# Attention in one tiling of four 64x64 tiles, with the softmax division inside the transposes

## The chip, the cores and the metric

One core of a Trainium2 chip runs the whole program. The metric is the device time of one execution in microseconds: median 962.74 us before the change, three runs between 958.96 and 964.65.

## The reference

The program is one attention layer and two mixture-of-experts layers. The change lies in the attention; q, k and v have 4 batches x 8 heads, 576 positions and 64 elements per head.

```python
scores = scale * np.matmul(q, k.transpose(0, 1, 3, 2))
log_f = np.log(np.clip(f, 0.0001, 1.0))
cum = np.cumsum(log_f, axis=-1)
decay = cum[:, :, :, None] - cum[:, :, None, :]
scores = np.where(causal, -1000000000.0, scores + decay)
scores = scores - np.max(scores, axis=-1, keepdims=True)
attn = np.exp(scores)
attn = attn / (np.sum(attn, axis=-1, keepdims=True) + 1e-09)
return np.matmul(attn, v).astype(np.float32)
```

## The kernel before, in words

The 32 heads are taken in 16 pairs p; the two heads of a pair lie in the two halves of the 128 partitions. The queries of a head are five tiles (QT, L29): tile 0 has 64 rows, tiles 1 to 4 have 128, and tile i needs only the first 64, 192, 320, 448 or 576 keys. 1600 key columns a head in all.

**Scores, qk (L119).** Per tile and head, an f32 product of 64 contraction rows fills 64x128 of TensorE's array, and a bf16 product (f32 for pair 0) adds the decay of the keys. An f32 product appears in the profile as two records, a bf16 product and an f32 transpose as one. VectorE takes the scores out of PSUM, adds the causal mask and finds the row's extreme (L151; tile 4 in two halves of 288 columns), ScalarE makes the exponential in place and the row sum (L159).

**Transposes, tr (L166).** The attention weights are transposed in blocks of 128x128 by TensorE's transpose (L175, L185, L190, L192), in four groups g, and copied out by ScalarE and VectorE (L177, L196, L198). **Products with v, av (L201)** use 128x64 or 64x64 of the array and gather in two PSUM tiles.

**Division.** rb (L209) inverts the row sums on VectorE, rt (L215) transposes them, writes them to DRAM (rd, L224) and reads them back as a broadcast over the partitions (rb, L226). xout (L228) copies the result out of PSUM on ScalarE and VectorE, multiplies it by that broadcast on GpSimd (L235) and splits it into two parts for the next layer (L237, L238).

**Order.** run (L240) writes TensorE's order out by hand: within iteration p, the transposes and products with v of pair p stand between the scores of pair p+1. The orders of the other engines and of the DMA queue on SyncE are a planner's. The load of q and k for pair p+2 and the weight fetches of the next layer are issued only after the broadcast of pair p (issue_after, L255). Every second iteration from p=3 to p=13, a block of the next layer's weights is decoded (L319) on ScalarE, VectorE and GpSimd; two small router weights (gw, L443) are loaded by code that stands behind the attention.

PSUM holds four score tiles, two transpose tiles and two result tiles, of one bank each.

Of the kernel before, what the change touches and what calls it, by code (L numbers as in the profile page):

```python
# [29 lines left out]
EO = {1: 0, 3: 192, 2: 640, 4: 960}  # L30
TQ = [None, (1, 2, 3, 4), (2, 3, 4), (3, 4)]
AV = [[(0, 0, 64, 0, 256, 0, 64), (0, 64, 64, 0, 256, 1, 0)],
# [3 lines left out]
NP = B * H // 2  # L36
PE = mybir.EngineType.PE


class Attention:  # L40
    def __init__(self, tc, ctx, cst, io, xth, xtl):
        self.tc, self.nc, self.cst, self.io = tc, tc.nc, cst, io
        self.xth, self.xtl = xth, xtl
        nc = self.nc
        dr = ctx.enter_context(tc.tile_pool(name="at_dr", bufs=1, space=DRAM))
        self.cd = dr.tile([B * H, 3, S], BF16, name="cd")
        self.rd = [dr.tile([10, 128], F32, name=f"rd{p}") for p in range(NP)]
        self.raw = ctx.enter_context(tc.tile_pool(name="at_raw", bufs=3))
        self.vp = ctx.enter_context(tc.tile_pool(name="at_v", bufs=2))
        self.ep = ctx.enter_context(tc.tile_pool(name="at_e", bufs=4))  # L50
        self.ap = ctx.enter_context(tc.tile_pool(name="at_a", bufs=2))
        self.xp = ctx.enter_context(tc.tile_pool(name="at_x", bufs=3))
        self.sm = ctx.enter_context(tc.tile_pool(name="at_sm", bufs=6))
        fix = ctx.enter_context(tc.tile_pool(name="at_fix", bufs=1))
        self.ps_s = ctx.enter_context(tc.tile_pool(name="ps_s", bufs=4, space=PSUM))
        self.ps_t = ctx.enter_context(tc.tile_pool(name="ps_t", bufs=2, space=PSUM))
        self.ps_x = ctx.enter_context(tc.tile_pool(name="ps_x", bufs=1, space=PSUM))
        self.e0 = [fix.tile([128, 128], F32, name=f"e0_{i}") for i in range(4)]
        self.dk = [fix.tile([128, S], BF16, name=f"dk{i}") for i in range(2)]
        self.neg = fix.tile([128, 128], BF16, name="neg")  # L60
        self.rs = [fix.tile([128, 10], F32, name=f"rs{i}") for i in range(2)]
        self.rr = [fix.tile([128, 32], F32, name=f"rr{i}") for i in range(2)]
        for t in self.e0 + self.dk[::-1]:
# [4 lines left out]
        for t in self.rr:  # L68
            nc.gpsimd.memset(t, 0.0)
        self.mark = [None, None, None]  # L70
        self.R, self.V, self.E, self.T = {}, {}, {}, {}
# [11 lines left out]
    def decay(self, ft, cum, c8, pc):  # L83
# [12 lines left out]
        nc.vector.tensor_sub(pc[:, 2], cum, pc[:, 1])  # L96
        nc.sync.dma_start(out=self.cd, in_=pc)

    def warm(self, n):
        z = self.e0[0]  # L100
        tp = self.ps_t.tile([128, 512], F32, name="ps_t")
        for i in range(n):
            self.nc.tensor.matmul(tp[:, :128], z, z, start=True, stop=True)
# [6 lines left out]
    def vload(self, p):  # L110
        nc = self.nc
        v = self.V[p] = self.vp.tile([128, 2, 7, D], F32, name="v")
        nc.sync.dma_start(out=v, in_=self.io["vL"][2 * p:2 * p + 2].rearrange("a p j d -> p a j d"))

    def rows(self, p):
        ins = self.nc.sync.dma_start(out=self.dk[p % 2][61:67], in_=self.cd[2 * p:2 * p + 2].rearrange("a r s -> (a r) s"))
        self.mark[2] = self.mark[2] or ins

    def qk(self, p, i, later=False):  # L119
# [4 lines left out]
        rs = self.rs[p % 2]  # L124
        if p not in self.E:
            self.E[p] = [self.ep.tile([128, 1536], F32, name="e") for _ in range(2)]
        es = ([self.e0[2 * (p % 2) + a] for a in range(2)] if i == 0 else
              [e[:, EO[i]:EO[i] + w] for e in self.E[p]])
        mask = self.cst["mask"]
        off = 448 + m - w if m == 128 else 512  # L130
        b = 128 - m
        prev = [None, None]
        for lo, hi in [(0, w)] if w <= 512 else [(0, w // 2), (w // 2, w)]:
            n = hi - lo
            ps = [self.ps_s.tile([128, 512], F32, name="ps_s") for _ in range(2)]
            for c in range(2):
                for a in range(2):
                    h = 64 * a
                    x, y = r[h:h + 64, 0, q0:w], r[h:h + 64, 1, lo:hi]
                    if c and p:  # L140
                        x, y = self.neg[h:h + 64, :m], d[h:h + 64, lo:hi]
                    elif c:
                        x, y = self.cst["sel"][h:h + 64, :m], self.c8[h:h + 64, lo:hi]
                    nc.tensor.matmul(ps[a][b:, :n], x, y, start=c == 0, stop=c == 1, tile_position=(h, b))  # L144
            for a in range(2):
                mx = self.sm.tile([128, 1], F32, name="mx")
                o, x, y = es[a][b:, lo:hi], ps[a][b:, :n], mask[b:, off + lo:off + hi]
                if i in (1, 2):
                    o, x, y = (t.rearrange("p (b k) -> p b k", k=64) for t in (o, x, y))
                    o = o[:, ::-1]  # L150
                nc.vector.tensor_tensor_reduce(  # L151
                    out=o, in0=x, in1=y, scale=-0.125,
                    scalar=BIGF if prev[a] is None else prev[a][b:], op0=ALU.add, op1=ALU.min, accum_out=mx[b:],
                )
                prev[a] = mx
        def exps():
            for a in range(2):
                c = a * 5 + i
                nc.scalar.activation(es[a][b:, :w], es[a][b:, :w], ACTF.Exp, bias=prev[a][b:], scale=-1.0,  # L159
                                     accum_out=rs[b:, c:c + 1])  # L160

        if later:
            return exps
        exps()

    def tr(self, p, g):  # L166
        nc = self.nc
        ident = self.cst["ident"]
        es = self.E[p]
        if g == 0:  # L170
            tp = self.ps_t.tile([128, 512], F32, name="ps_t")
            for a, e in enumerate(es):
                for c, o in enumerate((EO[3] - 64, EO[4] - 64)):
                    c += 2 * a
                    nc.tensor.transpose(tp[:, 128 * c:128 * (c + 1)], e[:, o:o + 128], ident)  # L175
            th = self.ap.tile([128, 512], F32, name="ath0")
            self.mark[0] = nc.scalar.activation(th, tp, ACTF.Copy)  # L177
            self.T[g, 0], self.T[g, 1] = th[:, :256], th[:, 256:]
            return
        tps = [self.ps_t.tile([128, 512], F32, name="ps_t") for _ in range(2)]  # L180
        n = 320 if g == 3 else 512
        k0 = 128 * g - 64
        if g == 3:
            for a, tp in enumerate(tps):
                nc.tensor.transpose(tp[:, 256:320], self.e0[2 * (p % 2) + a][64:, :], ident[64:, 64:],  # L185
                                    tile_position=(64, 0))
        for tp, e in zip(tps, es):
            for c, i in enumerate(TQ[g]):
                o = EO[i] + (QT[i][0] - k0 if i < 3 else k0)
                nc.tensor.transpose(tp[:, 128 * c:128 * (c + 1)], e[:, o:o + 128], ident)  # L190
            if g == 2:
                nc.tensor.transpose(tp[:, 384:512], e[:, EO[4] + 448:EO[4] + 576], ident)  # L192
        for a, tp in enumerate(tps):
            th = self.ap.tile([128, n], F32, name=f"ath{g}")
            if g == 3 or a:
                self.mark[1] = nc.vector.tensor_copy(th, tp[:, :n])  # L196
            else:
                self.mark[0] = nc.scalar.activation(th, tp[:, :n], ACTF.Copy)  # L198
            self.T[g, a] = th

    def av(self, p, g):  # L201
        nc = self.nc
        v = self.V[p]
        for j, k0, k, o, n, x, d0 in AV[g]:
            for a in range(2):
                nc.tensor.matmul(self.X[x][64 * a:64 * a + 64, d0:d0 + n], v[k0:k0 + k, a, j],  # L206
                                 self.T[g, a][k0:k0 + k, o:o + n], start=g == 0, stop=g == 3, tile_position=(k0, 64 * a))

    def rb(self, p):  # L209
# [868 lines left out]
```

## Time and profile before

| what | value |
|---|---|
| profiled execution, device time | 968.61 us |
| its span, first to last instruction | 966.8 us |
| median of three runs | 962.74 us |
| TensorE busy | 935.5 us, 97% of the span |
| VectorE, ScalarE, GpSimd busy | 61%, 43%, 24% |
| mean granted TensorE clock | 0.986 of 2.4 GHz |
| attention, until the next layer's matmuls follow each other | 207 us |

A row with a start and a length is one or several instructions of one form in order of time; in brackets stands how long the engine was idle before it and what it waited for. A group is all instructions of a line and shape, with their busy time and mean length. Matmuls overlap: the next one starts before the record of the last one ends, so that the distance between starts tells more than the length.

### The profile page before, as it was taken

What the parts mean: (1) busy time and instruction counts of PE and PEld (TensorE: products, weight loads), DVE (VectorE), ACT (ScalarE), POOL (GpSimd) and SP (SyncE); (2) the same over time, 40 slices, a digit from 0 to 9 for tenths busy, and PEclk for the clock granted to TensorE, in tenths of its full rate; (3) what the DMA queues carried; (4) which work ended last, traced back from release to release, by engine and by line L of the source; (5) the groups of instructions that cost most, each with busy time, mean ns of one, the idle gap of its engine ahead of it and who ended that gap; (6) DMA issues with size and microseconds to landing.
All of it is one profiled execution on the core that took longest, in us unless ns stands there. A gap on an engine that the chain in (4) does not pass through costs nothing.

```text
span 966.8 us, 16505 instructions
## 1 busy us (share of the span) xinstructions
PE 935.5 (97%) x6288; PEld 843.8 (87%) x6288; DVE 593.3 (61%) x1420; ACT 411.9 (43%) x903; POOL 232.9 (24%) x205
## 2 busy tenths in 40 slices
PE   7999999899999999999999999999899999999995
PEld 5655665489999999999999999899799999999995
DVE  6677777546586469459458445677785566465421
ACT  5676767534442132123123122333364465465431
POOL 1244444433121011012012000000112654345122
PEclk9999999999999999999999999999799999999998
DMA  5444444312132012013002000011485666566300
GB/s 161 117 136 136 132 131 139 105 56 66 44 110 65 1 47 85 1 29 104 1 22 87 1 1 1 33 67 55 157 263 171 202 236 202 169 197 218 112 35 30
DMA packets 53088, 94.83 MB, mean 98 GB/s; under 512 B 5954, under 2 KB 27086, under 8 KB 53007
## 3 DMA queue, kind: packets, MB, share of 16 engines
q1 hardware_dynamic: 47503, 79.58, 27.1%
q0 software_dynamic: 5504, 14.17, 4.3%
q8 instruction: 50, 0.82, 0.4%
q14 instruction: 31, 0.25, 0.1%
HBM read 84.10 MB, written 10.16 MB: 97 GB/s over the span
## 4 chain that ended last, share of the span: by engine, by line
PE 73%; DVE 9%; issue 7%; DMA 5%; POOL 2%; ACT 2%; SPq 0%; POOLq 0%; DVEq 0%; ACTq 0%
PE ps_g L377 26%; PE ps_y L395 13%; PE m_psy L698 8%; PE m_psg L683 7%; PE ps_s L144 5%; PE ps_t L190 3%; DVE dt L327 2%; PE avx L206 2%; PE avy L206 2%; DMA raw<-w 1%; DMA rd<-rt 1%; DMA qk<-qk 1%; ACT e L159 1%; PE m_pst L648 1%; PE rt_ps L534 1%
## 5 line engine op out<-in xcount | busy, mean ns | idle before, releaser
L377 PE MATMUL ps_g<-xth,w 128*128 128x384 f32 (+1 forms) x1184 | 309.0, 331 | 0.0
L377 PEld LDWEIGHTS ps_g<-xth,w 128*128 128x128 f32 x1184 | 213.2, 188 | 0.6
L377 PE MATMUL ps_g<-xtl,w 128*128 128x384 f32 (+1 forms) x592 | 196.4, 332 | 0.0
L395 PE MATMUL ps_y<-hh,w 128*128 128x384 f32 (+1 forms) x592 | 160.9, 333 | 2.2 <-DVE y L401 2.2
L698 PE MATMUL m_psy<-h2h,w 128*128 128x304 f32 x512 | 115.9, 309 | 0.0
L683 PE MATMUL m_psg<-ygh,w 128*128 128x304 f32 x512 | 115.1, 307 | 0.4 <-ACT ygh L650 0.4
L340 POOL TENSOR_TENSOR w<-ds,w 128x512 fp32r<-128x512 f32 x36 | 49.2, 1368 | 262.9 <-ACT w L339 262.4
L377 PEld LDWEIGHTS ps_g<-xtl,w 128*128 128x128 f32 x592 | 111.3, 188 | 0.1
L395 PEld LDWEIGHTS ps_y<-hh,w 128*128 128x128 f32 x592 | 107.1, 188 | 4.3 <-DVE y L401 4.0
L610 DVE TENSOR_TENSOR w<-raw,w 128x1024 fp32r<-128x1024 f32 x64 | 76.6, 1222 | 42.2 <-ACT w L609 21.8
L159 ACT ACTIVATE e<-e,mx 128x320 f32<-128x320 f32 (+4 forms) x160 | 88.0, 552 | 33.0 <-DVE mx L151 32.5
L395 PE MATMUL ps_y<-hl,w 128*128 128x384 f32 (+1 forms) x296 | 97.9, 331 | 0.0
L384 ACT ACTIVATE hh<-hs 128x384 fp32r<-128x384 f32 (+1 forms) x74 | 38.2, 516 | 134.6 <-DVE hs L383 134.6
L382 DVE SCALAR_TENSOR_TENSOR hs<-hs,ps_g 128x384 f32<-128x384 f32 (+1 forms) x74 | 40.0, 540 | 83.5 <-ACT hs L381 83.5
L151 DVE CUSTOM_DVE_ANT_0 e<-ps_s,mask 128x320 f32<-128x320 f32 (+4 forms) x160 | 62.7, 429 | 43.6 <-PE ps_s L144 33.6
L698 PEld LDWEIGHTS m_psy<-h2h,w 128*128 128x128 f32 x512 | 86.8, 191 | 0.4
L683 PEld LDWEIGHTS m_psg<-ygh,w 128*128 128x128 f32 x512 | 85.6, 189 | 0.6 <-ACT ygh L650 0.5
L609 ACT ACTIVATE w<-raw 128x1024 fp32r<-128x1024 f32 x64 | 67.5, 1058 | 40.7 <-PE m_psg L683 17.6
L381 ACT ACTIVATE hs<-ps_g 128x384 f32<-128x384 f32 (+1 forms) x74 | 35.3, 478 | 102.2 <-PE ps_g L377 102.1
L401 DVE TENSOR_TENSOR y<-ps_y,y 128x384 f32<-128x384 f32 (+1 forms) x124 | 67.0, 541 | 19.1 <-PE ps_y L395 18.2
L698 PE MATMUL m_psy<-h2l,w 128*128 128x304 f32 x256 | 78.2, 306 | 0.0
L683 PE MATMUL m_psg<-ygl,w 128*128 128x304 f32 x256 | 77.3, 302 | 0.0
(308 smaller groups left out, 1514.1 us busy)
## 6 DMA issues: line engine op xcount, KB each, us to landing
raw<-w SPq DMA_DIRECT2D x64, 512.0 KB
qk<-qk SPq DMA_DIRECT2D x16, 576.0 KB
v<-vL SPq DMA_DIRECT2D x16, 448.0 KB
raw<-mg SPq DMA_DIRECT2D x12, 512.0 KB
raw<-mv SPq DMA_DIRECT2D x12, 512.0 KB
raw<-mo SPq DMA_DIRECT2D x12, 512.0 KB
rb<-rd SPq DMA_DIRECT2D x16, 288.0 KB
yd<-yr SPq DMA_DIRECT2D x18, 256.0 KB
```

Of the source, the lines that this page charges most:

```text
L144: nc.tensor.matmul(ps[a][b:, :n], x, y, start=c == 0, stop=c == 1, tile_position=(h, b))
L151: nc.vector.tensor_tensor_reduce(out=o, in0=x, in1=y, scale=-0.125, scalar=BIGF if prev[a] is None else prev[a][b:], op0=ALU.add, op1=ALU. ...
L159: nc.scalar.activation(es[a][b:, :w], es[a][b:, :w], ACTF.Exp, bias=prev[a][b:], scale=-1.0, accum_out=rs[b:, c:c + 1])
L340: nc.gpsimd.tensor_sub(lo, s3, hi.bitcast(F32))
L377: nc.tensor.matmul(ps[:, :n], w[:, k, fs], x[:, k], start=(k == 0 and c == 0), stop=(k == 3 and c == 2))
L382: nc.vector.scalar_tensor_tensor(s[:, :n], s[:, :n], 1.0, pss[0][:, :n], op0=ALU.add, op1=ALU.mult)
L395: nc.tensor.matmul(ps[:, :n], w[:, f, ds], h[:, f, :n], start=(f == 0 and c == 0), stop=(f == 1 and c == 2))
L401: nc.vector.tensor_add(y, ps[:, :n], y)
L609: nc.scalar.activation(hi, r, ACTF.Copy)
L610: nc.vector.tensor_sub(lo, r, hi.bitcast(F32))
L683: nc.tensor.matmul(ps[:, :C], w[:, k, fs], x[:, k], start=(k == 0 and c == 0), stop=(k == 3 and c == 2))
L698: nc.tensor.matmul(self.P[e][d][:, :C], w[:, f, ds], h[:, f], start=(u == 0 and f == 0 and c == 0), stop=(u == 3 and f == 1 and c == 2))
```

## The change

All matmuls of the attention now use a quarter of the array, 64x64, at one of four places (row half, column half). A score product of 128 queries becomes two of 64. A transposition becomes an ordinary f32 product of a 64x64 block of weights with a 64x64 diagonal that holds the reciprocal row sums (inv), so that it divides as well; blocks that the mask empties are left out: 45 blocks a head, in three groups (KB), where the row halves have 6 and 8, 7 and 8, 8 and 8 blocks, times two heads on the two column halves. Products with v alternate heads between row halves: av runs twice per group, with swap 0 in iteration p and with swap 1 in iteration p+1.

Score PSUM is two tiles of two banks (one for each of tiles 0 to 3, both for tile 4), transposes and results have one tile of two banks each. Tile 4 of the scores is one VectorE instruction of 576 columns. The DRAM round trip (rd, rb), rt and the GpSimd multiply are gone; GpSimd makes the diagonals in two steps (columns 0 to 5 for tiles 4, 3, 2; columns 6 to 9 for tiles 1 and 0). v is loaded as 288 KB a pair and not 448. The order of all five engines is now written out by hand, and the scores of tile 4 for pair p+2 close iteration p. The decode steps are spread over two iterations, ScalarE's logarithm table is asked for at the start, and the router weights are loaded within the next layer.

```diff
--- before.py
+++ after.py
...
+EO = [1536, 0, 192, 512, 960]
+COL = [8, 6, 4, 2, 0]
+KB = [(3, 4, 7, 8), (1, 2), (0, 5, 6)]
 NP = B * H // 2
-PE = mybir.EngineType.PE
+ENG = mybir.EngineType
+def rows_of(kb):
+
+    return [list(range((kb + 2) // 2, 5)) + [0] * (kb == 0), list(range(max((kb + 1) // 2, 1), 5))]
...
+        self.ps_s = pool("ps_s", 2, space=PSUM)
+        self.ps_t = pool("ps_t", 1, space=PSUM)
+        self.ps_x = pool("ps_x", 1, space=PSUM)
...
+        one = self.sm.tile([128, 1], F32, name="one")
+        nc.vector.memset(one, 1.0)
+        nc.scalar.activation(one, one, ACTF.Ln)
...
-        nc.vector.tensor_sub(pc[:, 2], cum, pc[:, 1])
+        nc.gpsimd.tensor_sub(pc[:, 2], cum, pc[:, 1])
+        self.load(1)
+        self.vload(0)
         nc.sync.dma_start(out=self.cd, in_=pc)
...
+        v = self.V[p] = self.vp.tile([128, 9, D], F32, name="v")
+        self.nc.sync.dma_start(out=v, in_=self.io["vL"][p])
...
+        wide = w > 512
+        n = w // 2 if wide else w
+        ps = [self.ps_s.tile([128, 2, 512], F32, name="ps_s") for _ in range(1 + wide)]
+        for j in range(1 + wide):
+            ks = slice(j * n, j * n + n)
...
+                    h = slice(64 * a, 64 * a + 64)
+                    o = ps[a][:, j] if wide else ps[0][:, a]
+                    for b in range(0, m, 64):
+                        x, y = r[h, 0, q0 + b:q0 + b + 64], r[h, 1, ks]
+                        if c and p:
+                            x, y = self.neg[h], d[h, ks]
+                        elif c:
+                            x, y = self.cst["sel"][h], self.c8[h, ks]
+                        nc.tensor.matmul(o[b:b + 64, :n], x, y, start=c == 0, stop=c == 1, tile_position=(64 * a, b))
+        mask = self.cst["mask"][:m, 448:512] if i == 0 else self.cst["mask"][:, 576 - w:576]
+        for a in range(2):
+            mx = self.M[p, i, a] = self.sm.tile([128, 1], F32, name="mx", bufs=10)
+            o = self.E[p][a][:m, EO[i]:EO[i] + w]
+            x, y = (ps[a][:, :, :n] if wide else ps[0][:m, a, :n]), mask
+            if wide:
+                o, y = (t.rearrange("p (j n) -> p j n", j=2) for t in (o, y))
+            nc.vector.tensor_tensor_reduce(out=o, in0=x, in1=y, scale=-0.125, scalar=BIGF, op0=ALU.add, op1=ALU.min,
+                                           accum_out=mx[:m])
+
+    def exp(self, p, i):
+        m = QT[i][1]
+        w = QT[i][0] + m
+        for a in range(2):
+            c = COL[i] + a
+            e = self.E[p][a][:m, EO[i]:EO[i] + w]
+            self.nc.scalar.activation(e, e, ACTF.Exp, bias=self.M.pop((p, i, a))[:m], scale=-1.0,
+                                      accum_out=self.rs[p % 2][:m, c:c + 1])
+
+    def inv(self, p, c0, c1):
+        nc = self.nc
+        if p not in self.D:
+            self.D[p] = (self.dp.tile([128, 10, 64], F32, name="d"), self.sm.tile([128, 10], F32, name="r"),
+                         self.sm.tile([128, 10], F32, name="rr"))
+        d, r, rr = self.D[p]
+        nc.gpsimd.tensor_scalar_add(r[:, c0:c1], self.rs[p % 2][:, c0:c1], 1e-9)
+        nc.vector.reciprocal(rr[:, c0:c1], r[:, c0:c1])
+        sh = [128, c1 - c0, 64]
+        nc.gpsimd.tensor_tensor(d[:, c0:c1], self.cst["id2"].unsqueeze(1).to_broadcast(sh),
+                                rr[:, c0:c1].unsqueeze(2).to_broadcast(sh), op=ALU.mult)
+
+    def tr(self, p, g, ps=None):
+        nc = self.nc
+        tp = (ps or self.ps_t).tile([128, 2, 512], F32, name="ps_s" if ps else "ps_t")
+        es, d = self.E[p], self.D[p][0]
+        jobs, self.at = [[], []], {}
+        for kb in KB[g]:
+            for r, tiles in enumerate(rows_of(kb)):
+                self.at[kb, r] = len(jobs[r]), tiles
+                jobs[r] += [(kb, i) for i in tiles]
+        for n in range(8):
+            for r in range(2):
+                if n >= len(jobs[r]):
+                    continue
+                kb, i = jobs[r][n]
+                h = slice(64 * r, 64 * r + 64)
+                for c in range(2):
+                    a = (c + kb) % 2
+                    o = EO[i] + 64 * kb
+                    nc.tensor.matmul(tp[64 * c:64 * c + 64, r, 64 * n:64 * n + 64], es[a][h, o:o + 64],
+                                     d[h, COL[i] + a], start=True, stop=True, tile_position=(64 * r, 64 * c))
...
+        ns = [64 * len(j) for j in jobs]
+        for r in range(2):
+            o, x = th[:, r, :ns[r]], tp[:, r, :ns[r]]
+            if r == (g != 2):
+                nc.scalar.activation(o, x, ACTF.Copy)
             else:
+                nc.vector.tensor_copy(o, x)
+
+    def av(self, p, g, swap):
...
+        for kb in sorted(KB[g], key=lambda kb: (kb // 2 if g else (kb - 1) // 2, kb)):
+            for r in range(2):
+                t = r ^ swap
+                n0, tiles = at[kb, t]
+                if not tiles:
+                    continue
+                a = (r + kb) % 2
+                h, lo = slice(64 * r, 64 * r + 64), tiles[0] - 1
+                hi, w = lo + len(tiles), self.W[t, a]
+                for u0, u1 in list(self.parts(lo, hi, w)):
+                    m0 = 64 * (n0 + u0 - lo)
+                    nc.tensor.matmul(x[64 * a:64 * a + 64, t, 64 * u0:64 * u1], v[h, kb],
+                                     th[h, t, m0:m0 + 64 * (u1 - u0)], start=not w, stop=swap == 1 and kb in (5, 6),
+                                     tile_position=(64 * r, 64 * a))
+                    w.update(range(u0, u1))
...
-        nc.scalar.activation(xt[:, :320], ax, ACTF.Copy)
-        nc.vector.tensor_copy(xt[:, 320:], ay[:, :256])
-        nc.gpsimd.tensor_mul(xt, xt, self.rbt)
+        nc.vector.tensor_copy(xt[:, 64:].rearrange("p (s t q) -> p t s q", s=4, t=2),
+                              x[:, :, :256].rearrange("p t (s q) -> p t s q", s=4))
+        nc.vector.tensor_copy(xt[:, :64], x[:, 0, 256:320])
...
+        with self.tc.manual_schedule(engines={ENG.PE, ENG.Activation, ENG.DVE, ENG.Pool, ENG.SP}):
+            self.decay(*dec)
+            self.rows(1)
             self.warm(WARM0)
+            for i in (4, 3, 2, 1, 0):
                 self.qk(0, i)
+                self.exp(0, i)
+            self.warm(WARM1)
+            self.inv(0, 0, 6)
+            self.qk(1, 4)
             for p in range(NP):
                 nx = p + 1 < NP
+                if p + 2 < NP:
+                    self.load(p + 2)
+                hook("load", p)
+                self.inv(p, 6, 10)
+                self.tr(p, 0)
+                if nx:
+                    self.exp(p + 1, 4)
+                    self.qk(p + 1, 3)
+                self.tr(p, 1)
+                if nx:
+                    self.exp(p + 1, 3)
+                hook("a", p)
+                if p:
+                    for g in range(3):
+                        self.av(p - 1, g, 1)
+                    self.xout(p - 1)
+                if nx:
+                    self.vload(p + 1)
+                    self.qk(p + 1, 2)
+                    self.exp(p + 1, 2)
+                hook("b", p)
+                self.tr(p, 2)
+                self.av(p, 0, 0)
+                self.av(p, 1, 0)
+                if nx:
+                    self.qk(p + 1, 1)
+                    self.inv(p + 1, 0, 6)
+                    self.exp(p + 1, 1)
+                self.av(p, 2, 0)
+                if nx:
+                    self.qk(p + 1, 0)
+                    self.exp(p + 1, 0)
                 if p + 2 < NP:
                     self.rows(p + 2)
+                    self.qk(p + 2, 4)
+            for i in range(2):
+                tp = self.warm(2)
+                if i == 0:
+                    nc.vector.tensor_copy(self.sm.tile([128, 10], F32, name="r")[:, :1], tp[:, 0, :1])
+            for g in range(3):
+                self.av(NP - 1, g, 1)
+            self.xout(NP - 1)
...
+        if eng:
+            eng.tensor_scalar(s, s, 2.0 ** -30, None, op0=ALU.is_ge)
         nc.vector.scalar_tensor_tensor(t, hv, -0x40000000, t, op0=ALU.bitwise_and, op1=ALU.bitwise_or)
+        yield
         nc.vector.scalar_tensor_tensor(t, lv, 29, t, op0=ALU.logical_shift_right, op1=ALU.bitwise_or)
+        yield
         tf = t.bitcast(F32)
         if eng:
-            eng.tensor_scalar(s, s, 2.0 ** -30, None, op0=ALU.is_ge)
             eng.tensor_mul(s, s, tf)
...
+                def hook(at, p):
+                    if at == "load":
+                        if p == 1:
+                            cst.rest()
+                        if p == H0:
+                            todo.extend(m1.parts(0))
+                        if p >= H0 and (p - H0) % 2 == 0 and todo:
+                            todo[0] = m1.fetch(todo[0][0]), *todo[0][1:]
+                    if at == "b" and p == H0:
+                        cst.split()
+                    if at == "a" and p > H0 and (p - H0) % 2 and todo:
                         dec.append(m1.decode(*todo.pop(0), eng=nc.gpsimd))
+                        next(dec[0])
+                    elif dec:
+                        for _ in zip(range(1), dec[0]):
+                            pass
+                        if at == "b" and (p - H0) % 2 == 0:
                             for _ in dec.pop():
                                 pass
 
...
+                        if (i, f) in ((3, 0), (8, 0)):
+                            with tc.issue_after(m1.mark[0].ins), tc.issue_after(m1.mark[1].ins):
+                                next(gates, None)
```

## Rows read from the trace of the kernel before

**Rows 1.** Busy time and granted clock in three stretches of time.
```profile
core 0: us, PE busy (x) PEld busy (x) DVE busy (x) ACT busy (x) POOL busy (x), PEclk, DMA share, GB/s
16.00:22.00 6.00, 5.08 (x22) 2.61 (x23) 2.14 (x9) 3.23 (x12) 0.00 (x0) 0.72 0.29 70
92.71:104.10 11.39, 11.39 (x100) 7.08 (x99) 7.66 (x32) 8.03 (x26) 3.49 (x3) 1.00 0.43 119
182.00:188.00 6.00, 3.10 (x27) 1.88 (x29) 1.88 (x9) 2.47 (x10) 1.45 (x2) 1.00 0.18 58
```

**Rows 2.** TensorE in order of time: start us, length us.
```profile
16.02 0.77 PE L175 MATMUL ps_t<-cst,e 128*128 128x128 f32 x3 [1.19 <-ACT e L159]
...
30.21 0.66 PE L175 MATMUL ps_t<-cst,e 128*128 128x128 f32 x4
...
52.86 0.55 PE L175 MATMUL ps_t<-cst,e 128*128 128x128 f32 x3
...
184.09 0.66 PE L175 MATMUL ps_t<-cst,e 128*128 128x128 f32 x4
...
187.79 0.81 PE L144 MATMUL ps_s<-qk 64*128 64x320 f32 x4 [2.90 <-DMA qk<-qk]
...
199.94 0.66 PE L175 MATMUL ps_t<-cst,e 128*128 128x128 f32 x4
...
207.06 0.44 PE L377 MATMUL ps_g<-xtl,w 128*128 128x384 f32 x1
```

**Rows 3.** TensorE in order of time, inside one iteration.
```profile
92.71 0.43 PE L206 MATMUL avx<-ath,v 64*64 64x256 f32 x2
92.73 0.43 PE L206 MATMUL avy<-ath,v 64*64 64x256 f32 x2
92.98 0.38 PE L206 MATMUL avx<-ath,v 64*64 64x256 f32 x2
...
103.08 1.09 PE L190 MATMUL ps_t<-cst,e 128*128 128x128 f32 x8
104.10 0.43 PE L206 MATMUL avx<-ath,v 64*64 64x256 f32 x2
```

**Rows 4.** Groups by form, 0 to 210 us: xcount | busy, mean.
```profile
L206 PE MATMUL avy<-ath,v 128*64 128x256 f32 x192 | 33.6, 385 | 1.6 <-DVE ath L196 1.6
...
L235 POOL TENSOR_TENSOR xt<-xt,rb 128x576 f32<-128x576 f32 x15 | 21.2, 1410 | 123.6 <-DMA rb<-rd 52.3 <-ACT xt L233 27.7 <-ACT e L159 22.3
...
L159 ACT ACTIVATE e<-e,mx 128x320 f32<-128x320 f32 x32 | 17.8, 556 | 21.1 <-DVE mx L151 20.9
...
L151 DVE CUSTOM_DVE_ANT_0 e<-ps_s,mask 128x320 f32<-128x320 f32 x32 | 14.5, 487 | 24.4 <-PE ps_s L144 24.4
...
L331 POOL TENSOR_SCALAR ds<-ds 128x512 f32<-128x512 f32 x6 | 9.3, 1548 | 0.5
...
L332 POOL TENSOR_TENSOR ds<-ds,dt 128x512 f32<-128x512 f32 x6 | 7.6, 1274 | 1.0 <-DVE dt L328 0.5
...
L206 PE MATMUL avy<-ath,v 128*64 128x128 f32 x64 | 6.2, 273 | 0.0
...
L328 DVE SCALAR_TENSOR_TENSOR dt<-raw,dt 128x512 int32<-128x512 int32 x6 | 4.8, 796 | 0.2
```

**Rows 5.** VectorE in order of time, in the same iteration.
```profile
103.18 0.63 DVE L151 CUSTOM_DVE_ANT_0 e<-ps_s,mask 128x448 f32<-128x448 f32 x1
...
103.73 0.62 DVE L151 CUSTOM_DVE_ANT_0 e<-ps_s,mask 128x448 f32<-128x448 f32 x1
...
104.28 0.69 DVE L196 COPY ath<-ps_t 128x512 f32<-128x512 f32 x1
```

**Rows 6.** SyncE's DMA issues in order of time, last iterations of the attention.
```profile
163.98 0.63 SPq L224 DMA_DIRECT2D rd<-rt  x1
176.26 0.51 SPq L226 DMA_DIRECT2D rb<-rd  x1
176.83 0.46 SPq L108 DMA_DIRECT2D qk<-qk  x1
177.38 0.28 SPq L116 DMA_DIRECT2D dk<-cd  x1
```

**Rows 7.** VectorE in order of time, at the start.
```profile
10.85 0.19 DVE L445 CAST gw<-gw 128x64 fp32r<-128x64 f32 x1 [0.56 <-DMA gw<-wo]
```

More of the change, by code (lines that the diff above doesn't have):

```diff
@@ L67, in __init__ @@
             nc.gpsimd.memset(t, 1.0)
[L68 to L71, printed above, removed]
+        self.R, self.V, self.E, self.M, self.D, self.T, self.X = {}, {}, {}, {}, {}, {}, {}
     def decay_load(self, pool):
@@ L123, in qk @@
         w = q0 + m
-        rs = self.rs[p % 2]
         if p not in self.E:
[L126 to L135, printed above, removed]
+            self.E[p] = [self.ep.tile([128, 1600], F32, name="e") for _ in range(2)]
@@ L144, in qk @@
[L144 to L166, printed above, removed]
-        nc = self.nc
[L168 to L196, printed above, removed]
-            else:
-                self.mark[0] = nc.scalar.activation(th, tp[:, :n], ACTF.Copy)
-            self.T[g, a] = th
@@ L202, in av @@
+    def av(self, p, g, swap):
         nc = self.nc
         v = self.V[p]
[L204 to L209, printed above, removed]
-        nc = self.nc
-        r = self.sm.tile([128, 10], F32, name="r")
-        nc.vector.tensor_scalar_add(r, self.rs[p % 2], 1e-9)
-        nc.vector.reciprocal(self.rr[p % 2][:, :10], r)
@@ L215, in rt @@
-    def rt(self, p):
-        nc = self.nc
-        self.X = self.ps_x.tile([128, 320], F32, name="avx"), self.ps_x.tile([128, 384], F32, name="avy")
-        tp = self.X[1][:32, 256:]
-        nc.tensor.transpose(tp, self.rr[p % 2], self.cst["ident"])
-        rt = self.sm.tile([32, 128], F32, name="rt")
-        nc.scalar.activation(rt, tp, ACTF.Copy)
-        rb = self.rbt = self.xp.tile([128, S], F32, name="rb")
-        d = self.rd[p]
-        nc.sync.dma_start(out=d, in_=rt[:10])
-        d = d.rearrange("(a i) q -> a (i q)", a=2)[:, 64:]
-        self.mark[2] = nc.sync.dma_start(out=rb, in_=d.unsqueeze(1).to_broadcast([2, 64, S]))
+        if p not in self.X:
+            self.X[p] = self.ps_x.tile([128, 2, 512], F32, name="avx")
+            self.W = {(t, a): set() for t in range(2) for a in range(2)}
@@ L238, in xout, with run @@
         nc.gpsimd.tensor_sub(self.xtl[:, f, sl], xt, self.xth[:, f, sl].bitcast(F32))
-    def run(self, extra, pool):
+    def run(self, hook, pool):
+        nc = self.nc
         dec = self.decay_load(pool)
@@ L243, in run @@
         self.cst.load()
-        self.decay(*dec)
-        self.vload(0)
-        self.load(1)
-        self.rows(1)
-        with self.tc.issue_after(self.mark[2].ins):
-            self.vload(1)
-        with self.tc.manual_schedule(engines={PE}):
+        with self.tc.manual_schedule(engines={ENG.PE, ENG.Activation, ENG.DVE, ENG.Pool, ENG.SP}):
+            self.decay(*dec)
+            self.rows(1)
             self.warm(WARM0)
-            for i in (2, 3, 4, 1, 0):
+            for i in (4, 3, 2, 1, 0):
@@ L277, in run @@
-                for g in range(2, 4):
-                    self.av(p, g)
+                if p + 2 < NP:
[14 more added lines that the diff above has]
+                    self.xout(p - 1)
@@ L414 @@
 P0, P1 = 1, 1
[L415 removed]
+H0, WARM0, WARM1 = 2, 10, 3
 BLK0 = [4, 5, 6, 7, 8, 10, 12, 14, 16, 20, 22]
```

125 lines of the change are left out of this document (39 added, 86 removed), and 3 rows, old and new, of the table AV.

## Prediction

> **What bounds the kernel now.** I read busy time by stretch first. In an iteration in mid attention TensorE is busy without a gap for all of 11.39 us, while VectorE, ScalarE and GpSimd are busy 7.66, 8.03 and 3.49 us [rows 1]. Iterations are told apart by their first transposes: the first takes 14.2 us (16.02 to 30.21), the two after it 11.3 each, the eleven from 52.86 to 184.09 take 131.2 us or 11.93 each, since every second one also decodes weights, the fifteenth takes 15.85, and 7.1 us go from the last one's start to the next layer's steady stream [rows 2]. Then I read why the late ones are longer. SyncE holds its queue 12.3 us between writing the reciprocals (163.98) and reading them back (176.26), and the loads of q and k stand behind that [rows 6]; TensorE then waits 2.90 us for them [rows 2] and is busy 3.10 of 6 us [rows 1].
>
> Inside an iteration I read distances between starts. Two av records of one tile, 256 columns, stand 0.27 us apart: 0.21 of streaming and 0.055 of weights that nothing hides [rows 3]. From 128 to 256 columns a record grows by 112 ns [rows 4], close to two cycles a column at 2.4 GHz, the level that a granted clock of 1.00 means; so an f32 product of two records streams 1.67 ns a column. Eight transposes and a change of tile shape take 1.02 us (103.08 to 104.10), 0.15 more than eight steps of the 109 ns that I read as one of them [rows 3]. By these the streams of an iteration are: scores 3.33 us (1600 columns, f32 plus a bf16 record that I take as one cycle a column), transposes 2.83 (26), products with v 2.67. That is 8.8; the other 2.6 are some thirteen changes of shape and exposed weight loads.
>
> **The change, TensorE's own work.** Four 64x64 products start within 20 ns of one another today (92.71 to 92.73) and their second records together [rows 3], so I take four at once. Scores keep 3.33. The new transposes are 8 deep in each group: 8 products x 2 records x 56 ns (53 of stream) = 0.9 us, 2.7 for three. Products with v: the fullest tile has 14 blocks of 64 columns with swap 1 (1.5 us) and 8, then 6, with swap 0 (0.85 and 0.64). With small rests the iteration is 0.9 tr0, 0.93 scores 3, 0.9 tr1, 1.5 av, 0.67 scores 2, 0.9 tr2, 0.85 av, 0.4 scores 1, 0.64 av, 0.17 scores 0, 1.2 scores 4: 9.06 us, 2.3 under today's. No shape changes.
>
> **What the hand order makes late.** With TensorE this short, chains through the other engines end later. Prices: a 448-column extreme on VectorE every 0.55 us (103.18, 103.73), a 512-column copy 0.69 long [rows 5]; about 1.05 ns a column between the 320-column form's 487 ns [rows 4] and 448, so 0.68 for 576, 0.28 for 192, 0.15 for 64. A hand-over costs 0.1, from TensorE 0.2, an estimate.
> - Before tr1: after scores 4, VectorE does two extremes (0.2+1.36), then the reciprocal that stands behind them (0.25); GpSimd's multiply of 256 columns follows. The trace has no such small one. Bounds: nothing, and the 1.27 of 512 columns; at the 2.1 ns a column between 512 and 576 [rows 4] I take 0.7. With hand-over 2.57, against 1.95 of tr0 and scores 3: a stall of 0.6.
> - Before the last av: from the end of the swap-1 av, xout's two copies (0.2, then 0.6 and 0.14: the 0.69 copy of [rows 5] less its overlap with the next; both are on VectorE now), an extreme (0.42), two exponentials of tile 2 (0.18+1.12 [rows 4]), ScalarE's copy (0.6, a little under VectorE's 0.69): 3.3, against 2.82 on TensorE. A stall of 0.5.
> - Scores 4 need both score tiles, so the extremes of tile 0 first: 0.65.
>
> With 0.1 before scores 3 the iteration is 10.9 us, 0.4 under today's 11.3. GpSimd loses the 1.41 multiply and gains 0.7 and 1.0; it has room, except in decode iterations. In the odd ones the 1.55 comparison [rows 4] stands on GpSimd ahead of the reciprocals, which hold VectorE's queue and so the extremes of tile 0 and scores 4; what scores 4 wait for anyway covers half of it: 0.8. In the even ones a VectorE step of 0.8 [rows 4] stands before the reciprocal: 0.75. So 11.7 there, against 11.93.
>
> SyncE: the two round-trip issues and their wait go. The load of v now waits for av of the pair before, with the decay rows and the next q and k behind it. Rows are wanted 4.9 us later; 288 KB of v at the 119 GB/s of the iteration [rows 1] are 2.4 us, so I cost it at nothing, and at up to 2 us an iteration if that cover is gone. Weight fetches run an iteration ahead.
>
> **The sum**, against the profiled execution's 968.6 us. Start: VectorE waited until 10.85 for the router weights [rows 7] that are gone, and the first iteration carries no swap-1 av; TensorE's clock was granted 0.72 from 16 to 22 us [rows 1], and I leave that. Iteration 1 begins near 25.7, not 30.2: −4.5 (bounds −2 and −6). Two plain iterations: −0.8. Eleven: 129 against 131.2, −2.2. The fifteenth has no scores 4 (1.2+0.65 less) and no wait for q and k: 9.8 against 15.85, −6. The last one carries one swap-1 av more (1.5) and the fills around it: +1.7. Together −11.8. The median shown is 5.9 below the profiled execution, and I take the gain off the median: 962.74−11.8, about **951 us**. Router weights in the next layer, decode's new cuts there and the table load are nothing: other work covers them, and without that cover they cost under 1 us.
>
> **The rivals.**
> - *The stalls are not there* (VectorE and GpSimd shorter than priced): 13 iterations at 9.06 rather than 10.9 are 24 less, 927. For it: TensorE is the only engine full now [rows 1]. Against: the three chains are of in-order instructions with prices from rows.
> - *Weight loads show* (slower). A transpose record streams 53 ns and needs a 64-column load of about the same 55 [rows 3], nothing to spare. If each stands alone, a group takes 1.75, not 0.9: 0.85 more at tr1, 0.25 and 0.35 at tr0 and tr2 beyond the stalls they fill, 1.45 an iteration, 14 times: 971. It decides from about half of it, 0.6 a group. Against: eight transposes in 1.02 us [rows 3] hide theirs.
> - *Products start one by one.* 56 to 64 records a group at about 25 ns are 1.6 us: 0.7 an iteration net, 961, no change. Against: starts within 20 ns for four [rows 3]. The Trainium skill (TensorE: Matmul & The Clock Gate, section "Wait — 56ns, not 53.3ns?") states that start-to-start never drops below about 25 ns however few the columns. By that rule this rival's 961 would come; by the row 951.
> - *The change doesn't do what it says*: column halves take turns in scores and products, 9 us an iteration more, near 1080. The av rows speak against it.
>
> **How the numbers follow.** Forecast 0.56 (its own range 943 to 958: the start's bounds and 0.3 us an iteration), stalls not there 0.20, weight loads 0.13, one by one 0.08, turns 0.03. A measurement of this kernel can tell about 0.5% from no change, 957.9 to 967.6. Faster: 0.20 and nearly all of the forecast, 0.72. Same: its edge, one by one, and some of the weight loads, 0.14. Slower: 0.14. The range takes in the second case with its start and one by one: 922 to 966.
>
> **What would show it.** Plain iterations of 10.9 us with TensorE idle for 0.5 to 0.65 three times: before tr1 for GpSimd, before the last av for ScalarE's copy, inside scores 4 for VectorE. Transposing groups of 0.9 us, with four starts within 30 ns. No wait for q and k near the end. The attention ending near 195 us. Wrong would be: groups of 1.5 us or more (second and third rivals), no stalls (first), a granted clock under 1.00 in mid attention, or TensorE waiting for the decay rows.

## The result and the profile after

The changed kernel takes **976.33 us** (median of five runs, 972.14 to 978.24) against 963.14 for the kernel before (five runs, 958.96 to 966.43): a ratio of 1.0131, 95% interval 1.0091 to 1.0171, 1.3% slower. Forecast was 951, and the range ended at 966. The profiled executions lie only 6.1 us apart (span 972.9 against 966.8), since that of before was 5.5 above its own median. All of it is in the attention: its last product with v starts at 215.1 us instead of 206.9 (this start is called the attention's end below). From the next layer's stream to the last gate product (ps_g) of the first expert layer it takes 470.3 us against 471.9.

The head of the profile after, busy time and the DMA queues:

```profile
PE 926.5 (95%) x9976; PEld 873.9 (90%) x9976; DVE 578.5 (59%) x1357; ACT 400.9 (41%) x872; POOL 242.1 (25%) x249
...
q8 instruction: 79, 1.29, 0.6%
```

TensorE in order of time, the first record of some iterations, and of the next layer's stream; these answer to [rows 2]:

```profile
15.66 1.16 PE L193 MATMUL ps_t<-d,e 64*64 64x64 f32 x56
...
27.18 0.28 PE L193 MATMUL ps_t<-d,e 64*64 64x64 f32 x4
...
39.08 0.28 PE L193 MATMUL ps_t<-d,e 64*64 64x64 f32 x4
...
51.10 0.28 PE L193 MATMUL ps_t<-d,e 64*64 64x64 f32 x4
...
190.71 0.29 PE L193 MATMUL ps_t<-d,e 64*64 64x64 f32 x4
...
202.75 1.16 PE L193 MATMUL ps_t<-d,e 64*64 64x64 f32 x56 [0.77 <-POOL d L172]
...
215.33 0.44 PE L403 MATMUL ps_g<-xtl,w 128*128 128x384 f32 x1
```

The first iteration has become 2.7 us shorter than in [rows 2] (11.5), but the next two take 11.9 and 12.0 instead of 11.3, and the eleven from 51.10 to 190.71 take 139.6 instead of 131.2. The fifteenth takes 12.0 instead of 15.85. Inside the second iteration, busy time (answering to [rows 1]) and TensorE where a step begins or waits:

```profile
27.18:39.08 11.90, 10.93 (x336) 9.05 (x332) 7.13 (x27) 7.35 (x23) 3.97 (x7) 1.00 0.36 110
```

```profile
28.61 0.98 PE L143 MATMUL ps_s<-qk 64*64 64x448 f32 x8
29.41 0.37 PE L143 MATMUL ps_s<-dk,neg 64*64 64x448 bf16 x4
30.54 1.04 PE L193 MATMUL ps_t<-d,e 64*64 64x64 f32 x56 [0.76 <-ACT th L201]
31.41 0.33 PE L224 MATMUL avx<-th,v 64*64 64x192 f32 x1
31.42 0.22 PE L193 MATMUL ps_t<-d,e 64*64 64x64 f32 x1
31.43 0.37 PE L224 MATMUL avx<-th,v 64*64 64x192 f32 x1
31.43 0.28 PE L193 MATMUL ps_t<-d,e 64*64 64x64 f32 x3
...
36.22 1.17 PE L224 MATMUL avx<-th,v 64*64 64x64 f32 x13
...
37.54 1.24 PE L143 MATMUL ps_s<-qk 64*64 64x288 f32 x6
```

The group tr1 takes 0.87 us (30.54 to 31.41), as forecast, and the clock is 1.00. But it begins after an idle 0.76 us that ends with ScalarE's copy (L201). The two copies of each group, ScalarE and VectorE in order of time:

```profile
29.80 0.60 ACT L201 ACTIVATE th<-ps_t 128x512 f32<-128x512 f32 x1 [2.78 <-DVE th L203]
32.41 0.60 ACT L201 ACTIVATE th<-ps_t 128x512 f32<-128x512 f32 x1 [0.50 <-DVE th L203]
35.59 0.57 ACT L201 ACTIVATE th<-ps_t 128x512 f32<-128x512 f32 x1
```

```profile
27.79 0.76 DVE L151 CUSTOM_DVE_ANT_0 e<-ps_s,mask 128x576 f32<-128x576 f32 x1 [1.43 <-PE ps_s L143]
...
28.48 0.75 DVE L151 CUSTOM_DVE_ANT_0 e<-ps_s,mask 128x576 f32<-128x576 f32 x1
...
29.15 0.17 DVE L170 RECIPROCAL rr<-r 128x4 f32<-128x4 f32 x1
29.24 0.53 DVE L203 COPY th<-ps_t 128x384 f32<-128x384 f32 x1
31.75 0.62 DVE L203 COPY th<-ps_t 128x448 f32<-128x448 f32 x1 [0.75 <-PE ps_t L193]
...
36.20 0.69 DVE L203 COPY th<-ps_t 128x512 f32<-128x512 f32 x1 [1.34 <-ACT th L201]
```

They read different halves of one PSUM tile and write different halves of one SBUF tile, yet each second copy starts when the first has ended: ScalarE after VectorE in the first two groups, VectorE after ScalarE in the third. In the first group it is worst: ScalarE has been idle for 2.78 us, the products' last record ends at 28.8, but VectorE's copy stands in its queue behind two 576-column extremes and a reciprocal. In the third group the products of the last av that read VectorE's half start only at 36.95, 0.06 us after its copy.

### The profile page after: what moved, and what is told of

The parts are those of the page before. It is cut to its first block, busy times and chain, and to the rows that moved or that the text cites. A ratio compares the mean times of both kernels' runs of the same rounds, so it can differ in the third digit from the quotient of the medians.

```text
span 972.9 us, 23689 instructions
## 1 busy us (share of the span) xinstructions
PE 926.5 (95%) x9976; PEld 873.9 (90%) x9976; DVE 578.5 (59%) x1357; ACT 400.9 (41%) x872; POOL 242.1 (25%) x249
## 3 DMA queue, kind: packets, MB, share of 16 engines
q8 instruction: 79, 1.29, 0.6%
## 4 chain that ended last, share of the span: by engine, by line
PE 69%; DVE 11%; issue 9%; POOL 5%; ACT 3%; DMA 2%; POOLq 0%; SPq 0%; ACTq 0%; DVEq 0%
PE ps_g L403 26%; PE ps_y L421 13%; PE m_psy L725 8%; PE m_psg L710 7%; PE avx L224 4%; PE ps_s L143 3%; PE ps_t L193 2%; DVE e L151 2%; DVE dt L352 2%; ACT th L201 1%; DMA raw<-w 1%; POOL xtl L245 1%; DVE dt L354 1%; POOL ds L351 1%; PE rt_ps L561 1%
## 5 line engine op out<-in xcount | busy, mean ns | idle before, releaser
L160 ACT ACTIVATE e<-e,mx 128x576 f32<-128x576 f32 (+4 forms) x160 | 88.1, 553 | 24.2 <-DVE mx L151 24.2
L151 DVE CUSTOM_DVE_ANT_0 e<-ps_s,mask 128x576 f32<-128x576 f32 (+4 forms) x160 | 71.3, 483 | 26.8 <-PE ps_s L143 26.3
L193 PEld LDWEIGHTS ps_t<-d,e 64*64 64x64 f32 x2880 | 59.9, 134 | 29.0 <-POOL d L172 25.6
L143 PE MATMUL ps_s<-qk 64*64 64x288 f32 (+4 forms) x704 | 77.7, 411 | 6.3 <-DVE mx L151 4.9
L193 PE MATMUL ps_t<-d,e 64*64 64x64 f32 x2880 | 64.0, 221 | 17.5 <-ACT th L201 16.1
```

The lines of the kernel that those rows point to most:

```text
L143: nc.tensor.matmul(o[b:b + 64, :n], x, y, start=c == 0, stop=c == 1, tile_position=(64 * a, b))
L151: nc.vector.tensor_tensor_reduce(out=o, in0=x, in1=y, scale=-0.125, scalar=BIGF, op0=ALU.add, op1=ALU.min, accum_out=mx[:m])
L160: self.nc.scalar.activation(e, e, ACTF.Exp, bias=self.M.pop((p, i, a))[:m], scale=-1.0, accum_out=self.rs[p % 2][:m, c:c + 1])
L193: nc.tensor.matmul(tp[64 * c:64 * c + 64, r, 64 * n:64 * n + 64], es[a][h, o:o + 64], d[h, COL[i] + a], start=True, stop=True, tile_positi ...
```

## The experiments

"Cut" means one tile per row half in place of one tile of two halves.

**e1: both tiles cut.**

```diff
-        tp = (ps or self.ps_t).tile([128, 2, 512], F32, name="ps_s" if ps else "ps_t")
+        tp = [self.ps_t.tile([128, 512], F32, name=f"ps_t{r}") for r in range(2)]
...
-        th = self.ap.tile([128, 2, 512], F32, name=f"th{g}")
+        th = [self.ap.tile([128, 512], F32, name=f"th{g}_{r}") for r in range(2)]
```

> Both the PSUM tile of a transposing group and its copy in SBUF are cut into one tile per row half. Theory S (the copy of the second half waits for the copy of the first, since both halves are one tile): the two copies run side by side, the third stall before tr1 falls from 0.8 to about 0.2 us, the second half of the last av no longer waits for VectorE, the plain iteration falls from 12.0 to about 11.0 us and the whole by about 15 us against the changed kernel, to about 961. Rival W (small products and their weight loads make it slow): nothing moves, 976. Rival R (the reciprocals behind the 576-column extremes hold tr1, as the prediction had it): at most the last av gains, 3 to 6 us.

Measured: 967.07 us (963.32 to 971.31), ratio to before 1.0011 [0.9989, 1.0033]; attention ends at 209.9. That is 9 us off the changed kernel's time, where 15 were expected. The second iteration takes 11.13 us instead of 11.90. In the third, TensorE before tr1 waits 0.29 us and for GpSimd's multiply, which the prediction had named:

```profile
40.70 1.04 PE L193 MATMUL ps_t<-d,e 64*64 64x64 f32 x56 [0.29 <-POOL d L172]
```

**e2 and e3: only the PSUM tile cut (first half of the diff), only the SBUF tile cut (second half).**

> Only the PSUM tile is cut into one per row half. If the wait comes from both copies reading one PSUM tile, all of the gain of the run with both cut is here (iteration about 11.0 us); if it comes from both writing one SBUF tile, ScalarE's copy still starts when VectorE's ends and the iteration stays at 12.0 us.

> Only the SBUF copy is cut into one tile per row half. If the wait comes from both copies writing one SBUF tile, the iteration is about 11.0 us; if it comes from the PSUM tile, 12.0 us and ScalarE's copy still starts when VectorE's ends.

Measured, one execution each: 966.63 us with attention's end at 207.8, and 976.40 with its end at 215.9. ScalarE's first copy of e2, then that of e3:

```profile
39.55 0.60 ACT L201 ACTIVATE th<-ps_t 128x512 f32<-128x512 f32 x1 [1.86 <-PE ps_t L193]
```

```profile
41.44 0.60 ACT L201 ACTIVATE th<-ps_t 128x512 f32<-128x512 f32 x1 [2.84 <-DVE th L203]
```

In e2 it waits for the products alone and runs ahead of VectorE's copy (40.01 there); in e3 nothing has changed. It is the shared PSUM tile that makes the two readers take turns. The turns are waits of the program: in the trace of the changed kernel the copy at 29.80 waits for a semaphore that VectorE's instructions raise, VectorE's copy at 36.20 for ScalarE's; in e2 ScalarE's copy waits for TensorE's and its own alone. The cut would also let TensorE begin a group whose one half is free, but in the second and third iteration of e2 tr1 starts whole (29.69, 40.85), so this is not where the gain there comes from.

**e4: reciprocals earlier.** The reciprocals of tiles 1 and 0 move from behind the two extremes of tile 4 to before them.

```diff
-                self.inv(p, 6, 10)
+                if p == 0:
+                    self.inv(p, 6, 10)
                 self.tr(p, 0)
...
+                if nx:
+                    self.inv(p + 1, 6, 10)
+                if p + 2 < NP:
                     self.qk(p + 2, 4)
```

> The reciprocals and diagonals of tiles 1 and 0 are made before the scores of tile 4, so that they don't stand behind two 576-column extremes on VectorE; the tiles stay whole. Theory S: tr1 is released by ScalarE's copy behind VectorE's, which moves by 0.1 us only: about 1.5 us in all. Theory R (the reciprocal chain holds tr1, as predicted): 0.6 us an iteration, about 8 us.

Measured, one execution: 973.61 us, the two plain iterations 0.06 shorter. GpSimd's multiply is done at 40.60, over 2 us before tr1, and the wait is still there:

```profile
42.90 1.04 PE L193 MATMUL ps_t<-d,e 64*64 64x64 f32 x56 [0.76 <-ACT th L201]
```

So in the changed kernel the chain that I had priced for this stall was not the one that set it.

**e7: hand order on TensorE alone**, as before the change, the planner ordering the other engines.

```diff
-        with self.tc.manual_schedule(engines={ENG.PE, ENG.Activation, ENG.DVE, ENG.Pool, ENG.SP}):
+        with self.tc.manual_schedule(engines={ENG.PE}):
```

> The changed kernel with only TensorE's order written by hand; the planner orders ScalarE, VectorE, GpSimd and SyncE as in the kernel before. PSUM tiles are whole. If the hand order of the other engines is a gain by itself: slower than 976 by 5 us or more. If it is part of the loss: faster, 970 or less. Theory S says that the wait between the two copies stays in either.

Measured, one execution: 1007.61 us, attention's end at 247.4, and the wait before tr1 is longer, 1.14 us. The hand order is a gain of 31 us, but most of it lies at the start: iteration 1 begins at 52.91 us instead of 27.18. There the planner runs the next layer's decode steps on GpSimd (from 15.17 us on), and TensorE waits 8.2 us for one of ScalarE's copies; from 26 to 52.9 us, busy for 11.5 of 26.9, its granted clock is 0.58, between the two levels of 1.2 and 2.4 GHz. Later iterations take 12.8 us.

**e5: a better order, on e1.** Scores 0 go ahead of the last av, the reciprocals for tiles 1 and 0 ahead of scores 4 (as in e4), the third group's copies ahead of the exponentials of tile 2.

```diff
-                    self.exp(p + 1, 2)
                 hook("b", p)
                 self.tr(p, 2)
+                if nx:
+                    self.exp(p + 1, 2)
...
-                self.av(p, 2, 0)
-                if nx:
                     self.qk(p + 1, 0)
                     self.exp(p + 1, 0)
+                    self.inv(p + 1, 0, 6)
+                self.av(p, 2, 0)
```

> On top of the kernel with both tiles cut: the scores of tile 0 come before the last av, the reciprocals of tiles 1 and 0 before the scores of tile 4, and the copies of the third group before the exponentials of tile 2. Theory S+O (what is left are three waits made by the written order): the plain iteration falls from 11.1 to about 10.2 us and the whole by about 12 us, to 953 to 957. Rival T (TensorE's own work in 64x64 products is longer than the 9.1 us that the prediction summed, and fills the iteration): the waits go but the iteration stays above 10.8, 962 or more.

Measured, one execution: 954.82 us, attention's end at 198.5; the second and third iterations take 10.27 and 11.02 us.

**e6: e5 with the decode steps behind the reciprocals** (none at the start of an iteration).

```diff
-                hook("b", p)
+                if p == 2:
+                    hook("b", p)
...
-                    elif dec:
+                    elif dec and at != "load":
```

> The kernel of the run before, and the decode's steps are moved: none at the start of an even iteration, and the comparison on GpSimd behind the diagonals. Theory S+O: the decode iterations fall from 11.8 and 12.5 to those of the plain ones, 6 times 0.8 and 6 times 0.7 less, about 8 us on top: 944 to 950 and faster than the kernel before by over 1%. Rival D (the decode's work itself, not its place, costs the time): no more than 2 us on top.

Measured: **951.28 us** (950.03 to 957.02), ratio to before 0.9892 [0.9858, 0.9927], 1.1% shorter; attention's end at 193.3. The eleven iterations with decode take 123.8 us instead of e5's 128.3, about half of what was expected. One plain iteration of e6 (26.18 to 36.45, 10.27 us) shows no idle time on TensorE. Its steps:

```profile
26.18 0.33 PE L193 MATMUL ps_t<-d,e 64*64 64x64 f32 x4
...
27.47 0.98 PE L143 MATMUL ps_s<-qk 64*64 64x448 f32 x8
28.27 0.37 PE L143 MATMUL ps_s<-dk,neg 64*64 64x448 bf16 x4
28.70 1.04 PE L193 MATMUL ps_t<-d,e 64*64 64x64 f32 x56
29.58 0.33 PE L224 MATMUL avx<-th,v 64*64 64x192 f32 x1
...
30.95 0.49 PE L143 MATMUL ps_s<-qk 64*64 64x320 f32 x2
...
31.68 0.22 PE L193 MATMUL ps_t<-d,e 64*64 64x64 f32 x2
...
32.71 0.33 PE L224 MATMUL avx<-th,v 64*64 64x192 f32 x1
...
33.56 0.60 PE L143 MATMUL ps_s<-qk 64*64 64x192 f32 x8
...
34.11 0.25 PE L224 MATMUL avx<-th,v 64*64 64x64 f32 x1
...
35.14 0.70 PE L143 MATMUL ps_s<-qk 64*64 64x288 f32 x6
...
36.45 0.28 PE L193 MATMUL ps_t<-d,e 64*64 64x64 f32 x2
```

It still holds waits. On VectorE and GpSimd (last row) stand:

```profile
26.64 0.76 DVE L151 CUSTOM_DVE_ANT_0 e<-ps_s,mask 128x576 f32<-128x576 f32 x1
...
28.00 0.55 DVE L203 COPY th<-ps_t 128x384 f32<-128x384 f32 x1
...
34.67 0.35 DVE L151 CUSTOM_DVE_ANT_0 e<-ps_s,mask 128x192 f32<-128x192 f32 x1
```

```profile
35.57 0.83 POOL L172 TENSOR_TENSOR d<-mask,rr 128x384 f32<-128x384 f32 x1 [0.57 <-DVE rr L170]
```

These end at 27.40, 28.55, 35.02 and 36.40, and what needs the tile that each frees or fills starts 0.05 to 0.15 us later: scores 3 at 27.47, tr1 at 28.70, scores 4 at 35.14, tr0 at 36.45. In the trace TensorE's instructions at these four places wait for semaphores that VectorE's and GpSimd's raise. No idle time shows, since a matmul's record runs on past its last column (0.37 us for 448 bf16 columns, whose stream was priced at 0.19). By the distances between starts, three of the waits cost 0.10, 0.23 and 0.18 us, and inside scores 4 the second head starts 0.23 us after the first, when VectorE has read tile 0: an estimate of 0.5 to 0.7 us in all.

**e9: the order of e6 without the cut tiles** (the edits of e5 and e6 on the changed kernel).

> The changed kernel with the order of e6 (scores 0 ahead of the last av, reciprocals ahead of scores 4, copies of the third group ahead of the exponentials of tile 2, decode steps behind the reciprocals), but with the transposes' PSUM tile in one piece as in the changed kernel. Theory S+O (two separate losses): the copies still take turns, so the iterations are some 0.5 to 0.8 us longer than those of e6 and attention ends near 202: about 960. Rival: the better order hides the turns of the copies as well, so that it lies within 2 us of e6, 951 to 953.

Measured, one execution: 958.79 us, attention's end at 202.1; the wait before tr1 stays:

```profile
40.01 1.04 PE L193 MATMUL ps_t<-d,e 64*64 64x64 f32 x55 [0.76 <-ACT th L201]
```

So there are two losses that nearly add: the cut alone brings 9 us (976.3 to 967.1), the order alone 17.5, both 25. That both together end at the forecast's 951 is chance: the forecast counted stalls of 1.85 us an iteration, and put a kernel without them at 927.

**e10: e6 without the bf16 products.**

```diff
-            for c in range(2):
+            for c in range(1):
```

> The kernel of e6 without the bf16 products that add the decay to the scores (that part of the computation is left out). It measures their cost on TensorE by itself. As the prediction priced them (one cycle a column, 1600 columns: 0.67 us an iteration) scores 3 shorten by 0.19 us and plain iterations, which TensorE fills, by at most 0.7: attention ends 7 to 10 us earlier, about 942. Theory M (TensorE's sum was 1.1 us too small because these products and their changes of type cost over twice that): scores 3 shorten by 0.4 or more, plain iterations by over 1 us until another engine bounds them, 930 to 938. If neither shortens much, the missing 1.1 us lies in the products with v and the groups.

Measured, one execution: the time of the whole (1113.47 us) says nothing, as the layers behind the attention get other data. The attention ends at 188.3, 5 us earlier than in e6 and less than expected; the second iteration takes 9.99 us (24.16 to 34.15) instead of 10.27. It doesn't measure the bf16 products there, since tr1 starts 0.15 us after VectorE's copy in either run (26.47 and 28.55), with a wait that now shows:

```profile
26.62 1.04 PE L193 MATMUL ps_t<-d,e 64*64 64x64 f32 x56 [0.26 <-DVE th L203]
...
28.87 0.49 PE L143 MATMUL ps_s<-qk 64*64 64x320 f32 x2
...
29.46 1.21 PE L193 MATMUL ps_t<-d,e 64*64 64x64 f32 x63
```

Scores 2, which wait for nothing in either run, take 0.59 us here and 0.73 in e6 (30.95 to 31.68). The bf16 products of 320 columns cost 0.14 us; I had priced them at 0.13. They are not where TensorE's sum went wrong.

**e8: the weight fetch later, on e6.** It was meant to tell what stands behind the pauses that are left in e6 (last section).

```diff
-                        if p >= H0 and (p - H0) % 2 == 0 and todo:
+                    if at == "a" and p >= H0 and (p - H0) % 2 == 0 and todo:
+                        with tc.issue_after(at_.mk.ins):
                             todo[0] = m1.fetch(todo[0][0]), *todo[0][1:]
```

> The kernel of e6 with one thing moved: the fetch of the next weight block (512 KB, every second iteration) is issued only after ScalarE's copy of the second transposing group, instead of at the start of the iteration together with v and q, k. In e6 TensorE pauses in which it waits for nothing that the profile shows: 1.21 us before 105.41 and 1.67 us before 127.89, in the first group of the iterations that begin with the 512 KB burst, and the profile's DMA part lists a queue of kind 'instruction' with 16 KB packets. Theory I (TensorE's instructions come late behind the burst): the pauses of over 1 us at the start of those iterations go or follow the burst to a later place in the iteration; attention ends some 2 to 5 us earlier, near 946 to 949 against 951. Theory N (the pauses lie in the program and not in the traffic): they stand at the same products with the same lengths, 951.

Measured: 950.37 us (947.18 to 951.36), ratio to before 0.9865 [0.984, 0.989], the same as e6 within the noise; in the profiled execution the attention ends at 190.4, 2.8 us earlier. SyncE issued the two fetches at 98.00 and 121.49 us instead of 99.49 and 121.62: 1.49 and 0.13 us earlier, just as the iterations themselves (91.43 instead of 92.92, 115.12 instead of 115.25). The burst did not move within the iteration, so this run decides nothing on the traffic. The run shows something else, below.

## Why the prediction was wrong

The waits came at the three places named, though the first two end with another copy than forecast; four products run side by side, and decode costs what was priced. One step is shown to have failed; another sum came out longer, in part for want of waits that it didn't hold.

**The step that failed: "a stall of 0.6" before tr1 and "a stall of 0.5" before the last av.** Neither chain has one copy of a group waiting for the other: the first holds no copy at all, the second only ScalarE's. They take turns. In the second iteration of the changed kernel tr1 begins 3.36 us after tr0 (27.18 to 30.54), where the priced chain gave 2.57 (its terms with the hand-over add to 2.61; the hand-over of 0.1 was a guess, and 0.05 to 0.15 was measured); the priced chain itself was done earlier, with the end of GpSimd's multiply at 30.02 us, while ScalarE's copy ends at 30.40. In the third group VectorE's copy ends at 36.89, after ScalarE's, where ScalarE's was to be the last. Shown by e2 against e3: cutting the PSUM tile alone gives back 9.7 us, cutting the SBUF tile nothing. Without the turns e1's second iteration takes 11.13 us, 0.8 less than the 11.90 of the changed kernel and 0.2 above the forecast 10.9.

**The sum that came out longer: TensorE's 9.06 us.** By the steps of e6 an iteration is 10.27: tr0 1.29 (0.9 forecast), scores 3 1.23 (0.93), tr1 0.88 (0.9), av 1.37 (1.5), scores 2 0.73 (0.67), tr2 1.03 (0.9), av 0.85 (0.85), scores 1 and 0 0.55 (0.57), last av 1.03 (0.64), scores 4 1.31 (1.2). The six steps in which nothing waits (tr1 to scores 0) take 5.41 us, and 5.39 were priced. All of the excess lies in the other four, and each of them ends with one of the waits above. So 10.27 is not TensorE's own work but a bound on it; with the 0.5 to 0.7 us of waits taken off, some 9.5 to 9.8 are left, an estimate, and what makes the rest the runs do not separate. Where tr0 begins while scores 4 still run, the line between the two steps is rough.

The turns are 9 to 10 of the 25 us between forecast and measurement. In e1 the attention still ends 15 us behind the forecast, mostly in the iterations with decode (137.5 us, 129 forecast), the fifteenth (11.8, 9.8) and the last. The order of e6 takes much of this away, as e9 shows, but which wait it was in each place was not traced.

**Point by point.**
- The start: iteration 1 begins at 27.18, not 25.7; the first iteration waits for the same copies. A gain of 3.0 instead of 4.5; without the turns (e1) it begins at 26.56.
- Two plain iterations: 23.9 us, not 21.8.
- Decode: 12.8 and 12.56 in turn, 0.9 and 0.7 above the first plain one; +0.8 and +0.75 were forecast. Eleven take 139.6, not 129, all of it from the plain part.
- Fifteenth iteration: 12.04, not 9.8. No wait for q and k is left, as forecast, but the copies' turns and a decode step make the wait before tr1 1.42 us, and the next tr0 waits 0.77 for GpSimd.
- The last: 12.58 us (202.75 to 215.33), not 8.8. Its gaps are filled with matmuls of the next layer and the warm products, 1.61 us twice (203.85 to 205.46, 212.04 to 213.65).

Start 1.5, plain 2.1, eleven 10.6, fifteenth 2.2 and last 3.8 make 20.2: from the forecast end near 195 to 215.3. These are places, not causes.

**The rivals.** Weight loads don't show: groups of 0.87 us. Products don't start one by one: tr1 is 60 records in 0.87 us, 15 ns each, and four products start from 31.41 to 31.43. The Trainium skill (TensorE: Matmul & The Clock Gate, section "Wait — 56ns, not 53.3ns?") has starts never closer than about 25 ns; by it 60 of them would take 1.5 us, an estimate, and over the four places of the array the trace disagrees. Column halves don't take turns. The slower side came by a mechanism that was in no rival.

## What to carry to other kernels

Where two engines shall empty halves of one PSUM tile, give each its own tile, and look in the profile whether the second copy's idle time ends with the other copy instead of with the product. When an order is written by hand, follow every copy back to what stands ahead of it in its own engine's queue: here an idle ScalarE waited 2.8 us for a copy on VectorE behind two long extremes. And don't take an iteration without idle time in the rows for the engine's own work: compare the start of each step with the end of the instruction on another engine that frees its tile. Here 0.05 to 0.15 us lay between them four times.

## What the runs showed of the hardware

The shared tile itself was unexpected: the program lets the second reader of a PSUM tile wait for the first, though the two read different banks (e2 and the semaphores of the trace). With a tile each the two copies overlap: 39.55 to 40.15 and 40.01 to 40.53 in e2.

In e6 and e8 TensorE pauses inside a group with nothing to wait for. First e6, then e8, TensorE in order of time:

```profile
105.41 0.51 PE L193 MATMUL ps_t<-d,e 64*64 64x64 f32 x15 [1.21 <-issue]
...
127.89 0.80 PE L193 MATMUL ps_t<-d,e 64*64 64x64 f32 x36 [1.67 <-issue]
```

```profile
105.28 0.51 PE L193 MATMUL ps_t<-d,e 64*64 64x64 f32 x15 [2.25 <-issue]
...
126.39 0.81 PE L193 MATMUL ps_t<-d,e 64*64 64x64 f32 x37 [0.30 <-issue]
```

They stand behind the same record of the group in both kernels (the 35th of one group, the 14th of another), with other lengths: 1.21 and 2.25, 1.67 and 0.30 us. That speaks for the supply of instructions: the changed kernel moves 79 packets of 16 KB in the instruction queue, and has 2 x 9976 matmuls and loads, about 250 to a packet, where before there were 50 packets and 2 x 6288; a group runs through its 120 in 0.9 us. In all four pauses TensorE goes on 1.35 to 1.45 us after such a packet has ended (at 104.05 and 126.49 in e6, 103.93 and 124.94 in e8, by the packet times in the traces). In e8 one such packet moves while TensorE stands still:

```profile
q8 instruction: 1, 0.02, 2.6%
```

(the DMA queues from 102.9 to 105.2 us). It starts at 102.96, just after the weight block's burst has run from 98 us on; whether the burst held it back, or the packet is late for another reason, was not tested. That the pauses are waits for these packets is argued from the times, not shown by an edit.
